# Third weight matrix: its sums made in the first pass, two stores left out, and an issue order tied

## The chip, the core and the metric

The kernel runs on one core of a Trainium2 chip. The metric is the device time of one execution in microseconds (us). Three timed runs of the kernel before gave 975.1, 977.63 and 981.88 us, median 977.63 us.

The engines named below: PE (TensorE matmul; PEld is its weight load), DVE (VectorE), ACT (ScalarE), POOL (GpSimd), and SP (SyncE), whose queue issues every transfer of this kernel. Each engine works through its own queue in order.

## The reference

Attention over 8 batches, 8 heads, 576 tokens, head size 64, with keys and values averaged over groups of 8 tokens; its output, as 4608 rows of 512, goes through a gated feed-forward layer of width 1536.

```
k_p, v_p = mean over 8 tokens of k, v
attn     = softmax(q @ k_p.T / sqrt(64))          # 72 keys per head
x        = (attn @ v_p) as [4608, 512]
gate     = sigmoid(x @ w_gate);  val = x @ w_val  # [4608, 1536] each
out      = (gate * val) @ w_out                   # [4608, 512]
```

## The kernel before, in words

**Numbers as pairs.** Every operand of a large product is split into a high part and the rest (`split`, L164): ACT copies to the rounded type, DVE subtracts. A product then takes three matmuls (high-high, rest-high, high-rest). The weights come as 64-bit words that `to_f32` (L179) turns into 32-bit floats with two ACT and three DVE instructions per tile.

**Blocks.** The 4608 rows are 12 blocks of 384. Blocks 0 and 1 are done in `first_pass` (L850 on) with plain products: `whole` (L631, PE line L645) for gate and value, `accumulate` (L1133) for the third product. Blocks 2 to 11 are done in five pairs with a scheme of seven products for eight, for which sums and differences of matrix quarters are needed, of weights as well as of x and of h. A pair runs through `hidden` (PE line L605: gate and value products, with the attention of the blocks after next between them) and then `second_sums` (PE line L825: the third product, 7 x 3 units).

**Weights on their way.** In the first pass each weight tile is loaded, converted and split; the parts are stored to device memory for the later pairs (`keep_parts` for gate and value, `keep_o` for the third matrix). `keep_parts` stores four quarter parts per tile pair, among them number 8, the parts of the quarter W12, which `reload` never reads: it counts `n = sum(m != 8 ...)`. The converted weights themselves are stored too (`keep_whole`, `keep_w`), because the sums of quarters are made from them later. For the third matrix this is `sums("O", p)` (L262 to L281), called for p = 0 to 5 in the first pair: it loads `keptwO` back (512 KB), makes four differences on DVE (L270 to L272), splits them in two halves (ACT L166, DVE L167) and stores four parts (`keptS`, 256 KB each). `second_sums` reads `keptO` and `keptS` back as its weights.

**What sets the order.** Inside `first_pass` the string `ORDER` is the program: each word is one step (`conv.0.2` one instruction of a weight conversion, `sc.0.1` the scores of block 0 and head pair 1, `keep`, `oconv`, `hshi`, `acc`, ...), and every engine's queue follows it. After it a scheduler orders each engine's queue by its own estimate of when things are ready; `in_turn` (L158), where `tied[0]` is set, pins an instruction behind everything written before it for its engine. In `second_sums` the generator `operands()` (L578) prepares the next pair's x: from unit 8 on, every second unit makes one of seven operands (addition L574, copy ACT L166, rest DVE L167). These are not pinned before, so the scheduler places them.

**Buffers.** `big` has four buffers of 8 KB per partition, in rotation: the 64-bit weight tiles, the third matrix's raw tiles (`load_o`), the first pass's split h (`hshi`, `hslo`), and its outputs. `opool` has four as well.

Of the kernel before, what the change touches and what calls it, by code (L numbers as in the profile page):

```python
# [65 lines left out]
vlo.1.0 max.0.1 first.1.0 conv.0.0 keys.1.0 first.0.2 conv.0.0 lr.1.0 lq.1.0 sc.0.0@1 conv.0.0 put.1.0 first.0.3
lk.1.1 first.1.2 keys.0.2 sc.1.0@2 exp.0.1 first.1.3 put.0.2 conv.0.0 sc.0.2@0 rsum.1.0 rhi.1.0 max.0.0 exp.0.0
lw.1.0 lq.1.1 first.2.0 first.3.0 keys.0.3 lk.1.2 put.0.3 lq.2.0 conv.0.0 conv.0.0 keys.1.1 put.1.1 sc.0.3@1 lw.0.1
lq.1.2 lr.1.1 max.0.2 lk.1.3 sc.1.1@3 sum.0.0 max.0.3 exp.0.2 rest.0.0 conv.0.0 main.0.1 conv.0.0 main.0.0
turn.0.0@0 rlo.1.0 conv.1.0 lv.1.1 lq.2.1 again.0.0 rturn.0.0@4 conv.1.0 conv.1.0 lq.1.3 turn.0.1@5 max.1.0 exp.0.3  # L70
keep.0.0 pv.0@6,7 sc.2.0@1 lk.3.1 hi.0.0 rcopy.0.0 max.1.1 exp.1.1 hi.0.1 exp.1.0 conv.1.0 vput.1.0 conv.0.1 sum.0.1
vhi.0.0 conv.1.0 kw.1.0 vhi.0.3 lo.0.0 main.0.2 rest.0.1 lo.0.1 keys.1.2 main.0.3 turn.0.3@5 sum.1.0 main.1.1
main.1.0 max.2.0 keys.1.3 again.0.1 rturn.0.1@2 rsum.1.1 turn.0.2@0 put.1.2 vhi.0.2 vlo.0.2 conv.0.1 conv.1.0
vhi.0.1 sc.1.2@3 vlo.0.0 lq.2.3 rcopy.0.1 kw.0.0 rhi.1.1 rest.1.0 put.1.3 vlo.0.3 vlo.0.1 hi.0.3 hi.0.2 sc.2.1@4
sc.1.3@2 exp.2.0 lw.1.1 turn.1.1@6 vsum.1.1 lo.0.3 lk.3.0 lq.2.2 av.0.0@1 conv.1.0 again.1.0 turn.1.0@5 max.1.2
exp.1.2 lo.0.2 conv.1.0 keep.1.0 sc.2.3@0 hi.1.0 max.1.3 keys.3.1 x.0.0 exp.1.3 lq.3.1 av.0.2@3 x.0.2 conv.0.1
av.0.3@1 x.0.3 av.0.1@7 x.0.1 rturn.1.0@2 sc.2.2@3 rcopy.1.0 max.2.1 keys.3.0 xhi.0.1 put.3.1 put.3.0 xhi.0.0 lq.3.0
lo.1.0 av.1.0@2 vhi.1.1 rlo.1.1 conv.1.1 x.1.0 vput.1.1 sum.1.1 main.1.2 lw.0.2 conv.0.1 lv.1.2 rest.1.1 again.1.1
xlo.0.1 sc.3.1@7 hi.1.1 sc.3.0@1 lv.1.3 xlo.0.0 vlo.1.1 conv.0.1 main.1.3 turn.1.3@5 hi.1.3 lv.3.3 lw.1.2 exp.2.1
V.0.0@2 lk.3.2 lo.1.1 rturn.1.1@6 conv.0.1 lo.1.3 vsum.1.2 conv.0.0 rcopy.1.1 sum.2.0 lr.3.0 keep.0.1 conv.0.1  # L80
turn.1.2@5 max.2.3 av.1.1@4 vhi.1.2 x.1.1 rest.2.0 conv.1.0 hi.1.2 lo.1.2 kw.0.1 conv.1.1 vput.1.2 keep.1.1 max.2.2
vlo.1.2 conv.0.1 conv.1.1 G.0.1@6 G.0.0@4 vsum.1.3 lw.0.3 conv.1.1 keep.0.2 main.2.0 main.2.1 exp.2.3 exp.2.2
conv.0.1 keep.0.3 again.2.0 V.0.1@5 conv.1.1 gate.0.1 conv.0.2 lv.3.0 av.1.2@0 x.1.2 vhi.1.3 h.0.1 conv.1.1 conv.0.2
G.0.2@3 gate.0.2 conv.1.1 conv.1.1 vlo.1.3 kw.1.1 G.0.3@6 turn.2.1@5 hi.2.1 vput.1.3 conv.1.1 keep.1.2 keep.1.3
lw.1.3 conv.0.2 rturn.2.0@3 rcopy.2.0 lo.2.1 vsum.3.3 V.0.2@0 conv.0.2 av.1.3@5 turn.2.0@3 gate.0.3 lq.3.2 V.0.3@6
x.1.3 conv.0.2 h.0.2 av.2.1@0 hi.2.0 lo.2.0 av.2.0@3 conv.0.2 conv.0.2 keep.0.4 G.0.4@5 xhi.1.0 sum.2.1 xlo.1.0
xhi.1.1 xlo.1.1 keys.3.2 x.2.1 conv.1.2 conv.1.2 rsum.3.0 main.2.2 turn.2.2@0 x.2.0 conv.1.2 G.1.0@3 conv.0.2
gate.0.0 h.0.3 conv.1.2 conv.0.3 h.0.0 hi.2.2 kw.0.2 lk.3.3 lw.0.4 conv.0.3 gate.0.4 gate.1.0 G.1.1@4 V.1.0@6
max.3.1 lv.3.2 conv.1.2 kw.1.2 G.1.4@3 rhi.3.0 rlo.3.0 rest.2.1 main.2.3 conv.1.3 turn.2.3@5 h.1.0 conv.1.2 conv.1.2
conv.0.3 conv.0.2 put.3.2 max.3.0 conv.0.3 conv.1.2 conv.1.2 lw.1.4 conv.0.3 keys.3.3 keep.0.5 conv.1.3 keep.1.4  # L90
kw.0.3 V.0.4@6 h.0.4 exp.3.1 conv.1.3 lo.2.2 V.1.2@2 exp.3.0 conv.0.3 conv.0.4 lw.0.5 keep.1.5 conv.0.3 put.3.3
keep.0.6 G.1.5@7 conv.1.3 again.2.1 vsum.3.0 conv.0.4 gate.1.5 vput.3.0 conv.0.4 conv.1.3 V.1.4@1 conv.0.4 gate.1.1
V.1.1@0 h.1.1 conv.0.3 conv.0.3 V.1.5@7 h.1.5 kw.1.3 conv.1.4 lw.1.5 conv.1.3 conv.1.4 rturn.2.1@4 conv.0.4 hi.2.3
conv.1.4 sum.3.0 main.3.1 conv.1.3 G.1.2@6 main.3.0 G.1.3@0 rcopy.2.1 av.2.2@4 gate.1.2 h.1.2 sc.3.2@6 V.1.3@7
conv.1.4 conv.0.5 gate.1.4 ol.0 G.1.7@2 x.2.2 conv.1.3 conv.1.3 vput.3.1 conv.1.4 h.1.4 V.1.7@4 conv.0.5 G.0.5@1
conv.0.4 conv.0.4 conv.0.4 conv.0.5 lv.3.1 conv.1.5 conv.0.5 lq.3.3 lr.3.1 vsum.3.2 kw.0.4 conv.1.4 gate.1.7 ol.1
conv.1.5 rsum.3.1 h.1.7 oconv.0 oconv.0 V.0.7@2 oconv.0 keep.0.7 turn.3.0@4 kw.1.4 vsum.3.1 vhi.3.3 vhi.3.2 sc.3.3@3
keep.1.6 rhi.3.1 keep.0.8 rlo.3.1 vhi.3.0 gate.1.3 conv.0.5 ol.2 vput.3.2 G.0.7@0 lo.2.3 gate.0.5 h.1.3 conv.1.5
av.2.3@7 oconv.1 conv.0.4 hi.3.0 vhi.3.1 rest.3.0 conv.1.4 oconv.1 keep.0.9 kw.0.5 turn.3.1@5 conv.0.5 conv.1.5
# [1137 lines left out]
```

## Time and profile before

| | |
|---|---|
| timed runs | 975.1, 977.63, 981.88 us; median 977.63 us |
| the profiled execution | 978.66 us; its span 976.9 us |
| busy, share of the span | PE 96%, PEld 93%, DVE 72%, ACT 57%, POOL 5% |
| transfers | 251.10 MB, 257 GB/s over the span |
| stages by PE's lines | first pass's products to about 256 us; then five times `hidden` and `second_sums` |

The profile page gives for each engine the busy time, and a strip of 40 slices. The timeline gives single instructions with the idle time of their engine before them and, behind an arrow, what ended that idle time. A row of the windows view gives the busy time of each engine in one stretch. A busy PE row hides gaps shorter than a matmul's overlap with the next, since a matmul's end is modelled.

### The profile page before, as it was taken

How to read it: one execution, taken by the hardware profiler on the slowest of the kernel's cores; microseconds unless marked ns; L12 is line 12 of the kernel's file. 1: busy time of each engine (PE TensorE's matmuls, PEld its weight loads, DVE VectorE, ACT ScalarE, POOL GpSimd, SP SyncE). 2: the span in 40 equal slices, each digit the busy share in tenths (PEclk: the TensorE clock that was granted, in tenths of full speed). 3: DMA queues.
4: the chain of work that ended last, by engine and by line, in shares of the span. 5: the costliest groups of instructions: out<-in, count | busy, mean ns of one | idle time of the engine just before them, and what ended most of it. 6: DMA issues, size and time to landing. Idle time of an engine off the chain costs nothing.

```text
span 976.9 us, 15387 instructions
## 1 busy us (share of the span) xinstructions
PE 940.9 (96%) x5412; PEld 906.5 (93%) x5412; DVE 700.8 (72%) x1221; ACT 553.6 (57%) x1138; POOL 51.8 (5%) x67
## 2 busy tenths in 40 slices
...
GB/s 313 305 300 337 353 359 243 175 150 262 289 394 336 196 235 255 371 382 324 127 211 283 276 222 270 195 170 242 293 266 205 217 123 230 285 243 251 164 210 221
DMA packets 115068, 251.10 MB, mean 257 GB/s; under 512 B 11952, under 2 KB 49584, under 8 KB 113456
## 3 DMA queue, kind: packets, MB, share of 16 engines
...
q8 instruction: 43, 0.70, 0.3%
q14 instruction: 33, 0.27, 0.1%
HBM read 193.45 MB, written 56.62 MB: 256 GB/s over the span
## 4 chain that ended last, share of the span: by engine, by line
PE 71%; DVE 13%; DMA 10%; ACT 4%; issue 2%; SPq 1%; POOL 0%; DVEq 0%; POOLq 0%; ACTq 0%
PE chain L605 35%; PE acc L825 18%; PE chain L645 7%; PE acc L1133 5%; PE av L447 2%; PE sc L438 2%; DMA raw<-in_kT 1%; DVE hs L789 1%; DVE s L757 1%; DMA raw_o<-in_wo 1%; DMA w<-keptwO 1%; DMA w<-keptwV 1%; PE tp L526 1%; DMA raw<-in_wgv 1%; DMA keptwV<-w 1%
## 5 line engine op out<-in xcount | busy, mean ns | idle before, releaser
L605 PE MATMUL chain<-xo,parts 128*128 128x384 f32 x2352 | 441.7, 341 | 5.8 <-ACT sG L611 1.8
L605 PEld LDWEIGHTS chain<-xo,parts 128*128 128x128 f32 x2352 | 409.6, 188 | 10.6 <-ACT sG L611 2.4
L825 PE MATMUL acc<-hs,oparts 128*128 128x384 f32 x1260 | 229.3, 336 | 3.7 <-DVE hs L789 3.0
L825 PEld LDWEIGHTS acc<-hs,oparts 128*128 128x128 f32 x1260 | 218.1, 188 | 6.7 <-DVE hs L789 4.6
L645 PE MATMUL chain<-xo,parts 128*128 128x384 f32 x552 | 102.2, 340 | 2.8 <-DVE xo L1086 1.4
L617 DVE TENSOR_TENSOR y<-chain,sG 128x384 f32<-128x384 f32 x84 | 46.1, 553 | 77.3 <-ACT sG L611 26.2
L645 PEld LDWEIGHTS chain<-xo,parts 128*128 128x128 f32 x552 | 96.1, 188 | 4.2 <-DVE xo L1086 1.6
L617 DVE TENSOR_TENSOR y<-chain,sV 128x384 f32<-128x384 f32 x84 | 46.1, 551 | 35.1 <-PE chain L605 22.9
L789 DVE TENSOR_TENSOR hs<-h,hs 128x768 fp32r<-128x768 f32 x60 | 58.3, 979 | 16.6 <-ACT hs L788 16.5
L623 ACT ACTIVATE gate<-y 128x384 f32<-128x384 f32 x84 | 43.9, 525 | 41.2 <-DVE y L617 40.8
L788 ACT CAST hs<-h 128x768 fp32r<-128x768 f32 x60 | 50.1, 835 | 29.9 <-PE acc L825 29.4
L611 ACT COPY sV<-chain 128x384 f32<-128x384 f32 x84 | 40.0, 476 | 45.3 <-PE chain L605 42.5
L611 ACT COPY sG<-chain 128x384 f32<-128x384 f32 x84 | 39.9, 476 | 44.8 <-PE chain L605 44.2
L520 POOL TENSOR_TENSOR pm<-e,rz 128x384 f32<-128x384 f32 x32 | 31.3, 979 | 601.9 <-DVE rz L500 347.2
L788 ACT CAST hs<-s 128x768 fp32r<-128x768 f32 x45 | 37.0, 835 | 29.6 <-PE acc L825 21.4
L438 PE MATMUL sc<-kbd,raw 128*128 128x144 f32 (+1 forms) x280 | 47.6, 306 | 3.4 <-DMA raw<-in_qT 2.5
L1133 PE MATMUL acc<-oparts,hs 128*128 128x512 f32 x216 | 50.7, 391 | 0.0
L626 DVE TENSOR_TENSOR h<-y,gate 128x384 f32<-128x384 f32 x84 | 46.9, 562 | 1.7
L789 DVE TENSOR_TENSOR hs<-s,hs 128x768 fp32r<-128x768 f32 x45 | 42.4, 954 | 7.8 <-ACT hs L788 7.6
L438 PEld LDWEIGHTS sc<-kbd,raw 128*128 128x128 f32 (+1 forms) x280 | 37.3, 184 | 11.3 <-issue 4.0
L1133 PEld LDWEIGHTS acc<-oparts,hs 128*128 128x128 f32 x216 | 40.3, 188 | 8.0
L645 PE MATMUL chain<-xo,parts_x 128*128 128x384 f32 x216 | 40.2, 337 | 0.0
...
## 6 DMA issues: line engine op xcount, KB each, us to landing
...
oparts<-keptO SPq DMA_DIRECT2D x90, 256.0 KB, 3.8
...
raw<-in_vm SPq DMA_DIRECT2D x28, 256.0 KB, 4.7
...
```

The source lines that it names most:

```text
L438: nc.tensor.matmul(sc[lo - i * P:hi - i * P, i], lhsT=q[:, lo:hi], rhs=kbd[slot(b, p)], start=True, stop=True)
L520: nc.gpsimd.tensor_tensor(out=pm, in0=e[:, n, :, :KM], in1=rz[:, n, :, None].broadcast_to([P, 2 * QT, KM]), op=ALU.mult)
L605: nc.tensor.matmul(t, lhsT=w[:, h, a], rhs=x[:, y, c], start=(m in (1, 2, 5) and c == 0 and k == 0), stop=(c == 1 and k == 2), skip_group_ ...
L611: nc.scalar.copy(s, t)
L617: nc.vector.tensor_tensor(out=y, in0=t, in1=seen[kind, {2: 1, 3: 6, 7: 5}[m]], op=ALU.add)
L623: nc.scalar.activation(gates[q[0]][:, q[1]], y, AF.Sigmoid)
L626: nc.vector.tensor_tensor(out=hb[f // 4][:, f % 4, q[0] * BT:(q[0] + 1) * BT], in0=y, in1=gates[q[0]][:, q[1]], op=ALU.mult)
L645: nc.tensor.matmul(t, lhsT=w[:, c // 2, h, a], rhs=x[:, y, c % 2], start=(c == 0 and k == 0), stop=(c == NC - 1 and k == 2),)
L788: nc.scalar.copy(hs[:, 0], x)
L789: nc.vector.tensor_tensor(out=hs[:, 1], in0=x, in1=hs[:, 0].bitcast(F32), op=ALU.subtract)
L825: nc.tensor.matmul(acc[name, c], lhsT=w[:, k, h, c * P:(c + 1) * P], rhs=hs[:, y, k], start=(m in (1, 2, 5) and i % 3 == 0 and k == 0 and ...
L1133: nc.tensor.matmul(acc[i], lhsT=hss[f][:, y, a], rhs=oparts[f][:, w], start=(f == 0 and k == 0), stop=(f == NF - 1 and k == 2),)
```

## The change

1. `ORDER` is replaced as a whole. It has new words `osum` (a step of the sums of the third matrix) and `keeps` (their four stores), and no `keepw`.
2. `summed_o` makes the third matrix's sums from the two raw tiles while they are still in their `big` buffers; its result is a new `big` tile. One ACT copy and one DVE subtraction of four quarters take the place of two and two. The calls of `sums("O", ...)` in the first pair are gone, and with them the store and reload of `keptwO`.
3. `keep_parts` leaves out part 8.
4. In `second_sums` the steps of `operands()` run with `tied[0]` set.

```
 ORDER = """
-first.0.1 first.0.0 keys.0.0 first.1.1 keys.0.1 put.0.0 put.0.1 sc.0.1@0 lv.1.0 lw.0.0 lk.1.0 vsum.1.0 vhi.1.0
+first.0.0 first.0.1 keys.0.1 put.0.1 lv.1.0 keys.0.0 put.0.0 first.0.3 vsum.1.0 vhi.1.0 first.1.1 sc.0.1@0 first.0.2
...
     def keep_parts(kind, f):
         for k, m in enumerate(CHUNK[f % 2]):
-            keep(kind, f // 2, m, plain[kind, f][:, k])
+            if m != 8:
+                keep(kind, f // 2, m, plain[kind, f][:, k])
...
-    def keep_w(f):
-        w = raws_o.pop(f)[:, 2 * DM:].bitcast(F32)
-        for half in range(2):
+    def summed_o(p):
+
+        first, raw = raws_o.pop(2 * p), raws_o.pop(2 * p + 1)
+        w11, w12 = (first[:, 2 * DM:].bitcast(F32)[:, h * HALF:(h + 1) * HALF] for h in range(2))
+        w21, w22 = (raw[:, 2 * DM:].bitcast(F32)[:, h * HALF:(h + 1) * HALF] for h in range(2))
+        s = raw[:, :2 * DM].bitcast(F32).rearrange("p (m n) -> p m n", m=4)
+        nc.vector.tensor_tensor(out=s[:, 0], in0=w12, in1=w11, op=ALU.subtract)
+        nc.vector.tensor_tensor(out=s[:, 1], in0=w22, in1=w12, op=ALU.subtract)
+        yield
+        nc.vector.tensor_tensor(out=s[:, 2], in0=w22, in1=s[:, 0], op=ALU.subtract)
+        nc.vector.tensor_tensor(out=s[:, 3], in0=w21, in1=s[:, 2], op=ALU.subtract)
+        yield
+        t = sums_o[p] = big.tile([P, 4, 2, HALF], F32R, name="sums", tag="big")
+        nc.scalar.copy(t[:, :, 0], s)
+        yield
+        nc.vector.tensor_tensor(out=t[:, :, 1], in0=s, in1=t[:, :, 0].bitcast(F32), op=ALU.subtract)
+        yield
+
+    def keep_sums(p):
+        for k, m in enumerate((5, 7, 6, 4)):
             nc.sync.dma_start(
-                kept_w["O", f // 2][:, (half, 3 - half)[f % 2]], w[:, half * HALF:(half + 1) * HALF]
+                kept_s[m, p // 2][:, p % 2].bitcast(F32), sums_o[p][:, k].rearrange("p h n -> p (h n)").bitcast(F32)
             )
...
-            if i in (2,3,):
-                tied[0] = True
-                sums("O", made_o.pop(0))
-                tied[0] = False
...
-                    if (p, i) in ((0, 3), (0, 8), (1, 1), (1, 8),):
-                        sums("O", made_o.pop(0))
...
             if i >= 8 and i % 2 == 0:
+                tied[0] = True
                 next(build, None)
+                tied[0] = False
```

What moves on the engines, at three places. Line numbers after the change are some 10 to 30 higher than before.

**DVE, start of the first pass.** `TENSOR_REDUCE early<-h` and `early<-raw` (L943, then L954) are sums of keys, `early<-sc` (L957, L968) a maximum of scores, `w` and `raw` of 1024 elements the conversion of a weight tile. Before:

```order
2 L943 TENSOR_REDUCE early<-h 128x72 x2
3 L381 TENSOR_REDUCE small<-raw 128x64
4 L1050 TENSOR_TENSOR vl_105<-small,vh_100 64x64 x2
5 L957 TENSOR_REDUCE early<-sc 128x6
6 L943 TENSOR_REDUCE early<-raw 128x72
7 L194 TENSOR_SCALAR w_262<-w_262 128x1024
8 L943 TENSOR_REDUCE early<-h 128x72
9 L196 SCALAR_TENSOR_TENSOR raw_251<-raw_251 128x1024
10 L381 TENSOR_REDUCE small<-raw 96x64
```

After:

```order
2 L954 TENSOR_REDUCE early<-h 128x72 x2
3 L397 TENSOR_REDUCE small<-raw 128x64
4 L954 TENSOR_REDUCE early<-h 128x72 x2
5 L968 TENSOR_REDUCE early<-sc 128x6
6 L397 TENSOR_REDUCE small<-raw 128x64
7 L968 TENSOR_REDUCE early<-sc 128x6
8 L954 TENSOR_REDUCE early<-raw 128x72
9 L397 TENSOR_REDUCE small<-raw 96x64
10 L968 TENSOR_REDUCE early<-sc 128x6
```

The four key sums and three maxima of block 0 come first, and the first weight tile's conversion comes later (row 20). In both kernels the two subtractions that finish block 0's split x (L1086 before, L1097 after) are DVE's 77th and 78th instruction. SP loads accordingly: the first 1 MB weight tile is its 6th transfer before and its 16th after.

**ACT, first pair's `hidden`, the middle of it.** `sums` is the split of a sum of the third matrix, `sG` and `sV` the copies that empty a bank of products. Before:

```order
320 L611 COPY sV_3493<-chain 128x384
321 L611 COPY sG_3360<-chain 128x384
322 L166 CAST parts<-w_3282 128x256
323 L529 CAST ph<-tp 128x384
324 L166 CAST parts<-w_3149 128x256
325 L166 CAST sums<-s_3257 128x2x256
326 L611 COPY sG_3403<-chain 128x384
327 L166 CAST parts<-w_3282 128x256
```

After:

```order
332 L627 COPY sG_3288<-chain 128x384
333 L167 CAST parts<-w_3210 128x256
334 L410 ACTIVATE kbd_92<-ks 64x72
335 L639 ACT_TABLE_LOAD
336 L639 ACTIVATE gate_3342<-y 128x384
337 L167 CAST parts<-w_3093 128x256
338 L797 CAST hs<-h 128x768
339 L627 COPY sG_3331<-chain 128x384
340 L167 CAST parts<-w_3210 128x256
```

The twelve `sums` copies of the third matrix stand in this stretch before and none of them after; six copies of four quarters stand in the first pass instead. What the scheduler puts between the other instructions is different too: here a copy of h (`hs`) and a table load.

**DVE, third `second_sums` (the pair of blocks 6 and 7).** `hs` is the rest of an operand of the third products, `s_...<-h` and `h<-h` the additions for it; `s<-xs` (L574, then L590) an addition of x and `xo` the rest of an operand made of it. Before:

```order
863 L757 TENSOR_TENSOR s_7249<-h 128x768
864 L574 TENSOR_TENSOR s<-xs_6470 128x768
865 L757 TENSOR_TENSOR h<-h 128x2x384
866 L484 TENSOR_REDUCE m<-sc 128x6
867 L789 TENSOR_TENSOR hs<-s_7249,hs 128x768
868 L789 TENSOR_TENSOR hs<-s_6597,hs 128x768
869 L487 TENSOR_TENSOR e<-sc,m 128x432
870 L381 TENSOR_REDUCE ks<-raw 128x72
871 L789 TENSOR_TENSOR hs<-s_6597,hs 128x768
872 L167 TENSOR_TENSOR xo_7448<-s,xo_7448 128x768
873 L757 TENSOR_TENSOR s_7249<-s_7249,h 128x768
874 L757 TENSOR_TENSOR s_6597<-h,s_6597 128x768 x2
```

After:

```order
867 L798 TENSOR_TENSOR hs<-s_6525,hs 128x768
868 L766 TENSOR_TENSOR s_6525<-h,s_6525 128x768 x2
869 L798 TENSOR_TENSOR hs<-s_7177,hs 128x768
870 L798 TENSOR_TENSOR hs<-h,hs 128x768
871 L766 TENSOR_TENSOR s_7177<-h,s_7177 128x768
872 L798 TENSOR_TENSOR hs<-h,hs 128x768
873 L168 TENSOR_TENSOR xo_7333<-xs_6026,xo_7333 128x768
874 L798 TENSOR_TENSOR hs<-h,hs 128x768
875 L798 TENSOR_TENSOR hs<-s_6525,hs 128x768
876 L590 TENSOR_TENSOR s<-xs_6398 128x768
877 L798 TENSOR_TENSOR hs<-s_6525,hs 128x768
878 L812 TENSOR_TENSOR o<-acc,sG_7211 128x384
```

Before, the first addition of x stands at the head of the stage; after the change it stands behind more than eight operands of h, and the last operands of x (rows 897 and 898) stand behind the last outputs that DVE writes in the stage.

## Rows read from the trace of the kernel before

**Rows 1.** The page's head: span, then busy time, share and count of each engine

```profile
span 976.9 us, 15387 instructions
PE 940.9 (96%) x5412; PEld 906.5 (93%) x5412; DVE 700.8 (72%) x1221; ACT 553.6 (57%) x1138; POOL 51.8 (5%) x67
```

**Rows 2.** Windows: length, busy us of PE, PEld, DVE, ACT, POOL; clock, DMA

```profile
0.00:53.60 53.60, 32.15 (x171) 25.53 (x171) 41.80 (x79) 40.71 (x131) 10.59 (x27) 0.97 0.92 313
53.60:75.00 21.40, 20.91 (x130) 19.97 (x131) 19.27 (x35) 16.49 (x42) 1.86 (x2) 1.00 0.83 287
...
75.00:100.00 25.00, 24.77 (x143) 24.00 (x142) 24.82 (x39) 24.14 (x47) 2.83 (x2) 1.00 0.98 340
...
175.00:200.00 25.00, 25.00 (x128) 22.20 (x127) 15.11 (x22) 12.80 (x21) 0.00 (x0) 1.00 0.37 122
...
250.00:325.00 75.00, 73.21 (x441) 70.54 (x440) 70.90 (x152) 53.87 (x122) 8.12 (x6) 1.00 0.96 339
325.00:400.00 75.00, 75.00 (x447) 74.73 (x447) 64.38 (x102) 44.58 (x84) 3.32 (x4) 1.00 0.71 235
```

**Rows 3.** PE's waits over the whole span: engine, line, tile, releaser: us, times, longest

```profile
PE acc L825 <- DVE hs L789: 3.0, 5, 1.0
```

**Rows 4.** Timeline of PE to 57 us: start, us, instruction, idle before and its releaser

```profile
12.17 1.81 PE L438 MATMUL sc<-kbd,early 128*128 128x144 f32 x6 [2.03 <-DMA early<-in_qT]
...
53.60 2.21 PE L645 MATMUL chain<-xo,parts 128*128 128x384 f32 x11 [1.39 <-DVE xo L1086]
```

**Rows 5.** Timeline of DVE to 54 us, three of its idle times

```profile
2.63 0.28 DVE L140 CAST identr<-cst 128x128 fp32r<-128x128 f32 x1 [2.63 <-DMA cst<-in_const]
...
5.03 1.41 DVE L943 TENSOR_REDUCE early<-h 128x72 f32<-128x576 f32 x2 [2.11 <-DMA h<-in_kT]
...
45.85 0.75 DVE L943 TENSOR_REDUCE small<-raw 128x72 f32<-128x576 f32 x1 [2.47 <-DMA raw<-in_kT]
```

**Rows 6.** Groups by line: operation, tiles, shapes, count, busy us, mean ns, idle before

```profile
L270 DVE TENSOR_TENSOR s<-w 128x512 f32<-128x512 f32 x10 | 6.9, 687 | 6.1 <-DMA w<-keptwO 4.8 <-DMA w<-keptwV 1.3
...
L271 DVE TENSOR_TENSOR s<-w,s 128x256 f32<-128x256 f32 x10 | 4.8, 481 | 0.1
...
L272 DVE TENSOR_TENSOR s<-w,s 128x256 f32<-128x256 f32 x10 | 4.2, 417 | 0.0
...
L167 DVE TENSOR_TENSOR sums<-s,sums 128x512 fp32r<-128x512 f32 x20 | 14.2, 713 | 0.9 <-ACT sums L166 0.9
...
L166 ACT CAST sums<-s 128x512 fp32r<-128x512 f32 x20 | 12.4, 621 | 13.4 <-DVE s L270 3.7 <-DVE m L484 3.0 <-issue 2.4
...
L196 DVE SCALAR_TENSOR_TENSOR raw<-raw 128x1024 uint32<-128x1024 uint32 x12 | 14.7, 1228 | 0.0
...
L188 ACT ACTIVATE w<-raw 128x1024 f32<-128x1024 f32 x12 | 13.9, 1156 | 1.6 <-DMA raw<-in_wgv 1.6
...
L1133 PE MATMUL acc<-oparts,hs 128*128 128x512 f32 x216 | 50.7, 391 | 0.0
```

**Rows 7.** Timeline of ACT, then of PE, around 300 us, first pair's hidden stage

```profile
300.01 0.62 ACT L166 CAST sums<-s 128x512 fp32r<-128x512 f32 x1 [0.89 <-DVE s L270]
...
301.06 1.15 PE L605 MATMUL chain<-xo,parts 128*128 128x384 f32 x5 [1.33 <-ACT sG L611]
```

**Rows 8.** DMA issues: tiles, queue, count, KB each, median us to landing

```profile
keptS<-sums SPq DMA_DIRECT2D x24, 256.0 KB, 5.4
```

**Rows 9.** Timeline of DVE from 648 us, third pair's `second_sums`

```profile
649.74 0.95 DVE L574 TENSOR_TENSOR s<-xs 128x768 f32<-128x768 f32 x1
...
652.05 1.82 DVE L789 TENSOR_TENSOR hs<-s,hs 128x768 fp32r<-128x768 f32 x2
...
659.30 0.96 DVE L574 TENSOR_TENSOR s<-s,xs 128x768 f32<-128x768 f32 x1
```

**Rows 10.** Timeline from 200 us: last raw tile's load on SP, end of its conversion on DVE

```profile
200.55 0.33 SPq L311 DMA_DIRECT2D raw_o<-in_wo  x1
...
210.19 0.69 DVE L320 TENSOR_TENSOR oparts<-raw_o,oparts 128x512 fp32r<-128x512 f32 x1
```

More of the change, by code (lines that the diff above doesn't have):

```diff
@@ L64 @@
 ORDER = """
-first.0.1 first.0.0 keys.0.0 first.1.1 keys.0.1 put.0.0 put.0.1 sc.0.1@0 lv.1.0 lw.0.0 lk.1.0 vsum.1.0 vhi.1.0
[L66 to L99, printed above, removed]
@@ new lines @@
+conv.0.0 lw.0.1 rest.0.1 lo.0.0 lq.1.2 keys.1.3 kw.0.0 lr.1.1 rcopy.0.0 again.0.1 conv.1.0 main.0.2 main.0.3
+rturn.0.1@4 turn.0.3@3 conv.1.0 vhi.0.1 lq.2.1 vhi.0.3 sc.1.1@1 lq.2.2 hi.0.3 vhi.0.0 vhi.0.2 lo.0.1 conv.1.0
+rcopy.0.1 sc.2.0@0 keys.1.2 lk.3.1 put.1.2 conv.1.0 sc.1.2@4 vlo.0.3 lw.1.1 conv.0.1 conv.0.1 turn.0.2@2 conv.1.0
+put.1.3 vlo.0.0 max.1.1 exp.1.1 lo.0.3 keep.0.0 vlo.0.2 conv.0.0 max.1.2 vlo.0.1 keep.0.1 hi.0.2 rsum.1.1 max.2.0
+exp.1.2 conv.1.0 lq.3.0 sum.1.0 main.1.0 kw.1.0 main.1.1 av.0.0@3 sc.1.3@7 sc.2.2@1 sc.2.1@4 max.1.3 lq.2.3 put.3.0
@@ new lines @@
+h.1.0 G.1.2@7 conv.1.2 sc.3.2@1 conv.0.2 keep.0.5 keep.1.4 lo.2.2 G.1.5@0 rcopy.2.1 h.1.3 conv.0.3 kw.0.3 V.1.2@4
+keys.3.3 lo.2.3 av.2.3@2 av.2.2@5 conv.1.2 conv.1.2 conv.1.3 lq.3.3 exp.3.1 sum.3.0 conv.0.4 lv.3.2 V.1.5@6 conv.0.4
+conv.1.3 conv.0.3 lw.0.5 conv.0.3 keep.0.6 conv.1.3 rhi.3.1 conv.1.4 conv.0.3 keep.1.5 lw.1.5 gate.1.2 G.0.5@7 h.1.2
+rest.3.0 conv.0.4 conv.0.4 x.2.3 main.3.0 conv.1.3 conv.1.4 conv.0.3 V.1.4@2 turn.3.0@4 gate.1.5 conv.0.4 again.3.0
+keep.0.7 rturn.3.0@0 gate.1.4 x.2.2 main.3.1 turn.3.1@5 conv.0.5 ol.0 h.1.5 kw.0.4 conv.1.4 conv.0.5 G.0.4@6 h.1.4
```

82 lines of the change are left out of this document (53 added, 29 removed).

## The prediction, made before the changed kernel ran

> **What bounds the kernel now.** Read the page's head first [rows 1]: PE is busy 940.9 of 976.9 us, so at most 36.0 us of visible idle time can be won as long as the products stay the same, and they do: the change adds and removes no matmul. The question is where those 36.0 us lie and which of them the change reaches. The windows view, read by stage [rows 2], answers the first half. The first 53.6 us hold 21.45 of them, the 21.4 us behind those 0.49, 75 to 100 us 0.23; between 250 and 325 us there are 1.8, between 325 and 400 none. The list of PE's waits [rows 3] has, for the second half of the program, 3.0 us for h's operands (DVE), in five places of at most 1.0.
>
> In the start PE waits for DVE. The first product gets going at 53.60 us, released by the split of x on DVE [rows 4]. DVE was busy 41.80 of the 53.60 us before that [rows 2], so it stood idle for 11.8. Two views show where: 2.63 and 2.11 us for the first constants and the first k, 2.47 for a late k at 45.85 us [rows 5], the rest in small pieces, among them waits for scores, which PE made late because q landed behind other loads (2.03 us at 12.17 us, [rows 4]).
>
> **The change part by part.**
>
> *Start of the first pass: taken at -3.0 us, bounds -6 and +2.* The split of x is DVE's 77th and 78th instruction in both orders, and the mix is the same but for one more split of a 512-wide weight part, like the 0.71 us of L167 [rows 6], and one short instruction less: 0.5 more. So DVE's work ahead of PE's first product stays; what can change is its idle time. The first two k land as before, so 2.63 + 2.11 = 4.7 us stay. Then two more k and three q come before the first weight tile, and key sums and maxima of block 0 follow one another; of the other 7.1 us I leave 2.7, an estimate: some for the third k and the first maxima, the rest for the small gaps. That is 4.4 us less idle, less 0.5 more work: 3.9 if no wait like the 2.47 comes back, 1.4 if it does. Behind the start PE cannot run ahead at will: DVE is busy 24.82 of 25 us between 75 and 100 us [rows 2], with the same work per product. I take 3.0. The largest gain, -6, is nearly all of the 7.1 us, less the 0.5; the other bound, +2, is one new wait of the size seen (2.47) with no gain elsewhere but 0.5. The first weight tile comes later in SP's queue (16th, not 6th); its first ACT instruction (L188, [rows 6]) then stands in ACT's queue behind the exponentials of block 0, which do not need it, and before the second group's, which would be late if it were.
>
> *Rest of the first pass: 0, bounds -1 and +3.* The twelve stores of part 8 and the 24 stores of `keptwO` go from SP's queue; the 24 stores of `keptS` (256 KB, 5.4 us to landing, [rows 8]) come into it. None is on PE's path. DVE gets six sums: four subtractions of 256 elements at 0.42 to 0.48, 1.8 us, and a subtraction of 1024, bounded by 0.70 for 512 and 1.23 for another operation of 1024 [rows 6]; I take 1.2, since it is the same length. ACT gets six copies of 1024 at about 1.16 (L188, [rows 6]). That is 18 us of DVE and 7 us of ACT, at a time when there is room: between 175 and 200 us DVE was busy 15.11 and ACT 12.80 of 25 us, and transfers 0.37 [rows 2]. The cover is thin at one point, the last raw tiles, and this is the slower rival below.
>
> *Sums out of the first pair: taken at -2.5 us, bounds 0 and -4.2.* Six sums leave the stretch of 236 to 326 us: on DVE 6 x (0.69 + 0.48 + 0.42 + 2 x 0.71) = 18.1 us, on ACT 12 x 0.62 = 7.4 us [rows 6], and on the transfer queues 6 loads of 512 KB and 24 stores of 256 KB, 9.4 MB, while the transfers were busy 0.96 of the time [rows 2]. DVE was busy 70.90 of 75 us there; with about 15 of the 18 us gone it has less than the 64.38 of the next 75 us, in which PE never stood. What PE lost can be pointed at: at 300.01 us ACT begins a `sums` copy after 0.89 us of waiting for DVE's L270, the copy `sG` that empties a bank stands behind it, and PE idles 1.33 us [rows 7]. That is three quarters of the stretch's 1.8 us. PE's busy rows hide short gaps, though. Weight loads were busy 70.54 of 75 us in this stretch and 74.73 in the next, where the products have the same shape [rows 2]: by this the loss is 74.73 - 70.54 = 4.2 us. I take 2.5, between the two, because the queue of ACT after the change has new instructions in front of `sG`, as the order shows. What is late next, once DVE has room, is the bank copies behind PE itself. A table load more on ACT for each of two tables costs nothing while ACT is busy 54 of 75 us.
>
> The Trainium skill, in Trainium Kernel Development and Optimization, section Performance Expectations, says that matmul busy time is a bad measure of how close PE is to its limit, since matmuls are pipelined, and that the busy share of weight loads is the good one. By it this term would be -4.2 and the sum 1.7 us lower. The trace agrees in this stretch; in the whole span the rule would find 976.9 - 906.5 = 70.4 us, of which a part is not idle at all, as the third product of the first pass streams 512 columns per load.
>
> *x's additions tied: taken at -2.0 us, bounds -3.0 and +2.* Of PE's waits for h's operands (3.0 us in five places, [rows 3]) one is plain in DVE's timeline: before the `hs` at 652.05 us stands an addition of x of 0.95 us at 649.74, and another, of 0.96, at 659.30 among the next ones [rows 9]. Tied, all of them stand behind these operands, as the order shows. I take two thirds of the 3.0 because the last pair has no x to prepare and its waits stay. What the tie adds is a wait at the other end: the last operands of x are made after the stage's last outputs, and `hidden` of the next pair reads them. An operand costs an addition of 0.95 us, a rest of 0.91 (half of the 1.82 at 652.05, same shape, [rows 9]) and a copy on ACT of at most the 1.16 of 1024 elements [rows 6]; its first reader in `hidden` is PE's sixth product, some 6 us in, so I cost it nothing. If that cover were gone it would be up to 0.5 us at each of four borders, the +2.
>
> *What the scheduler does elsewhere: 0, within 2 us either way.* The later pairs keep their sums of gate and value, and the stretch from 325 to 400 us had nothing to lose to them [rows 2].
>
> *Sum.* -3.0 + 0 - 2.5 - 2.0 = -7.5. The profiled execution took 978.66 us (span 976.9), 1.0 above the median of the runs. 978.66 - 7.5 = 971.2; against the median, **970.2 us**.
>
> **Rivals.**
>
> *A. The start gives nothing.* DVE is filled to the limit from 50 to 100 us, and another late load stands in for the 2.47. For it: SP's queue is in order, and every move of a load delays others; against it: the q of block 0 are now ahead of all weights. Start 0, the rest as forecast, a little less: -4. Time 978.66 - 4 - 1.0 = 973.7. Chance 0.2.
>
> *B. PE loses more than its busy rows show, and gets it back.* By the weight loads the first pair's stretch gives 4.2, the start its full 3.9, the tie all 3.0, and scheduling chance 1: -12.1. For it: 74.73 against 70.54 [rows 2]; against: it needs all terms at their ends. Time 978.66 - 12.1 - 1.0 = 965.6. Chance 0.22. The Trainium skill's rule on weight loads, named above, is the rule behind it.
>
> *C. Slower: the raw tiles come late at the end of the first pass.* The sums now need a `big` buffer of their own, held until four stores land (5.4 us), and both raw tiles of a pair stay until the sums have read them. In rotation the 12th raw tile gets the buffer of h's ninth operand, so its load starts when PE has finished with that. From there PE has 36 matmuls of the third product at 50.7 / 216 = 0.235 us [rows 6], 8.5 us, and some 12 shorter ones, at most 2.8, before it needs the tile: 8.5 to 11.3 us, of which I take 10.7. Before, load and conversion of this tile took from 200.55 to 210.88 us, 10.3 us [rows 10]. Now a sum's 3.0 us of DVE and 1.2 us of ACT may stand in front. The 11th tile waits for stores to land as well. The point that decides is whether the chain exceeds 10.7 us: if a sum (3.0 + 1.2) and its stores (5.4) all come into it, PE waits 9.6 us. With the start at 0 and 2.5 us won later, 978.66 + 9.6 - 2.5 - 1.0 = 984.8. Against it: the order puts the last sum behind most of the conversion. Chance 0.08.
>
> **The numbers.** Forecast 970.2 us, chance 0.5, itself spread over 967 to 973. The range of 8 in 10 reaches from 964 (B and its half spread) to 978 (A and its half, short of C): **964 to 978**. One per cent, 9.8 us, is about what a measurement of this kernel can tell from no change. Below 967.9 lie most of B (0.19) and the lower end of the forecast (0.08): 0.27. Above 987.4 lies the upper end of C: 0.03. Within: 0.70.
>
> **What would show it.** In the changed profile the start is right if PE's first plain product starts near 50 us and DVE's idle time before it is near 7 us; wrong if a new DMA wait of over 2 us stands there. The sums are right if PE's idle time between 250 and 325 us is under 0.5 us and DVE's share there falls to that of the later pairs; the tie, if waits of line L825 (new number) for `hs` fall to about 1 us and no wait for `xo` appears at the border to `hidden`. A PE wait for `oparts` or `hs` before the first outputs, near 205 to 215 us, would be C. The prediction would be wrong altogether if the first products of blocks 0 and 1 were starved after 55 us: then several us of idle time would stand in the 21 us behind the first product, where 0.49 stood.

## The result, and the profile after

The changed kernel takes 982.41 us (median of 15 runs, 980.55 to 986.88); the kernel before, run on the same chip, 978.44 us (15 runs). The ratio is 1.003, with a 95% interval of 1.0016 to 1.0044: slower by 1.6 to 4.3 us, where 7.5 us less was forecast, and above the range's end of 978. (The medians differ by 4.0 us, the ratio says 2.9: it is not the quotient of the two medians.) The profiled execution took 982.51 us.

The page's head, beside [rows 1]:

```profile
span 980.7 us, 15323 instructions
PE 945.8 (96%) x5412; PEld 912.5 (93%) x5412; DVE 706.2 (72%) x1221; ACT 558.3 (57%) x1134; POOL 46.9 (5%) x67
```

PE's matmuls are as many, and it is "busy" for 4.9 us more. So more busy time does not mean less lost time here; part of the loss is inside it. The windows say where, beside [rows 2] (columns as there):

```profile
0.00:53.60 53.60, 35.51 (x179) 30.52 (x180) 45.64 (x82) 40.62 (x126) 9.21 (x27) 0.88 0.94 325
53.60:75.00 21.40, 20.71 (x133) 20.18 (x132) 19.99 (x39) 20.00 (x51) 4.09 (x4) 0.98 0.80 270
75.00:100.00 25.00, 25.00 (x150) 24.91 (x149) 22.63 (x34) 21.37 (x43) 2.83 (x2) 1.00 0.80 277
...
250.00:325.00 75.00, 71.33 (x423) 69.00 (x422) 54.74 (x122) 44.77 (x106) 4.99 (x6) 0.98 0.65 209
325.00:400.00 75.00, 75.00 (x447) 74.72 (x446) 63.13 (x101) 49.21 (x87) 4.08 (x4) 1.00 0.70 226
```

From 250 to 325 us DVE fell from 70.90 to 54.74 us and transfers from 0.96 to 0.65, as forecast, and yet PE did 423 matmuls where it had done 441. The list of PE's waits (engine, line, tile, releaser: us, times, longest) has new entries, and the one of [rows 3] is nearly gone:

```profile
PE chain L621 <- ACT gate L639: 2.3, 1, 2.3
...
PE chain L621 <- DMA parts<-keptG2B: 2.0, 2, 1.7
PE chain L621 <- DMA parts<-keptG3B: 1.8, 2, 1.5
...
PE acc L834 <- DVE hs L798: 0.3, 1, 0.3
```

PE now waits for weights (`keptG2B`, `keptG3B`) that it hardly waited for before, and for a gate on ACT.

**PE's lost time by stage.** To see losses shorter than a visible gap, and those of a slower clock, I took from each trace the time from one matmul's start to the next one's, less the usual time for that shape (the lower quartile over all profiles of this study), and added it up by stage. "hid" is a pair's `hidden`, "sec" its `second_sums`; "0-60" holds all time before PE's first matmul too. us:

```
                        0-60 60-h1  hid1  hid2  hid3  hid4  sec3  sec4 other  total  profiled time
before                  33.1   5.6   5.2   8.3   3.8   3.4   3.6   1.7   6.3   70.9  978.66
before, again (e14)     32.0   5.5   4.8   8.0   3.5   4.0   3.6   1.7   5.7   68.7  976.48
changed                 31.4   6.4   8.5   7.5   7.7   6.1   0.4   0.6   6.1   74.8  982.51
changed, again (e13)    30.0   6.6   7.5   7.5  11.3   6.5   0.4   0.6   6.0   76.5  984.23
e1 tie only             34.0   8.7   5.1   8.4   7.4   6.9   0.4   1.0   7.9   79.8  987.66
e2 untied               31.2   5.1   7.5   6.6   5.6   4.7   3.2   1.7   6.2   71.9  979.57
e3 sums again           29.6   6.4   3.9   9.7   4.0   6.9   0.4   0.6   7.1   68.7  976.36
e4 stores on POOL       30.8   5.9   5.7   7.5   9.9   5.8   0.4   0.6   5.2   71.9  980.08
e5 two stores           30.4   6.5   6.8   8.2   7.7   6.2   0.4   0.6   9.5   76.4  984.07
e6 two stores, untied   29.8   7.1   7.6   7.3   6.3   4.7   3.6   1.7   6.3   74.5  982.18
e7 again, untied        30.5   6.1   4.6  13.4   4.6   3.8   3.6   1.7   6.7   74.9  982.62
e8 no part 8            34.5   4.5   4.3   8.1   3.7   3.7   3.2   1.7   6.0   69.8  977.48
e16 no part 8, again    31.3   4.5   4.3   8.0   3.9   3.2   3.2   1.7   6.7   66.8  974.48
e9 one unit earlier     30.9   4.5   8.8   8.7   3.4   6.1   0.4   0.5   6.1   69.3  977.06
e10 earlier, no part 8  30.2   3.8   4.0   7.0   5.2   5.7   0.6   0.7   8.4   65.7  973.40
e11 part 8 stored       30.2   9.0   7.7   7.5   8.0   5.9   0.4   0.6   6.1   75.4  983.28
e12 earlier, POOL       31.0   5.3   4.8   7.9   3.8   7.1   0.8   0.5   6.2   67.4  975.58
e15 earlier, POOL again 31.2   4.9   5.5   7.9   3.7   7.2   0.7   0.6   8.1   69.7  977.83
```

Read the first four rows. The change wins about 2 us before 60 us and 4.3 in the third products of pairs 3 and 4. It loses 3 us in the first pair's `hidden`, and 6 to 10 in those of pairs 3 and 4, whose own code the diff leaves as it was. A row is one execution: the kernel before and e1 have the same order on PE, DVE and ACT up to 255 us, and yet lost 5.6, 5.5 and 8.7 us from 60 us to the first pair.

### The profile page after: what moved, and what is told of

The parts are those of the page before. It is cut to its first block, busy times and chain, and to the rows that moved or that the text cites. A ratio compares the mean times of both kernels' runs of the same rounds, so it can differ in the third digit from the quotient of the medians.

```text
span 980.7 us, 15323 instructions
## 1 busy us (share of the span) xinstructions
PE 945.8 (96%) x5412; PEld 912.5 (93%) x5412; DVE 706.2 (72%) x1221; ACT 558.3 (57%) x1134; POOL 46.9 (5%) x67
## 4 chain that ended last, share of the span: by engine, by line
PE 71%; DVE 12%; DMA 10%; ACT 5%; issue 2%; SPq 1%; DVEq 0%; ACTq 0%
PE chain L621 34%; PE acc L834 21%; PE chain L661 7%; PE acc L1149 3%; PE sc L454 3%; PE av L463 3%; DMA out<-o 2%; DMA parts<-keptG2B 1%; PE tp L542 1%; DVE raw L197 1%; DVE w L199 1%; DMA raw<-in_kT 1%; DMA parts<-keptG3B 1%; DVE parts L239 1%; DMA parts<-keptG4B 1%
## 5 line engine op out<-in xcount | busy, mean ns | idle before, releaser
L536 POOL TENSOR_TENSOR pm<-e,rz 128x384 f32<-128x384 f32 x32 | 29.1, 910 | 636.1 <-DVE rz L516 378.7
L797 ACT CAST hs<-s 128x768 fp32r<-128x768 f32 x45 | 37.3, 837 | 29.6 <-PE acc L834 22.0
```

Source lines behind the costliest of these rows:

```text
L797: nc.scalar.copy(hs[:, 0], x)
```

## The experiments

Medians, with the ratio to the kernel before on the same chip. Differences in the text are those of the ratios, times 978.4 us. Each interval reaches 1.2 to 2.5 us to either side, so two versions that differ by less than some 2 us are not told apart.

```
                        median us   ratio    95% interval
changed                  982.41    1.0030   1.0016 to 1.0044
e1 tie only              985.36    1.0076   1.0050 to 1.0102
e2 untied                979.16    1.0005   0.9992 to 1.0018
e3 sums again            976.31    0.9972   0.9954 to 0.9990
e4 stores on POOL        981.19    1.0034   1.0022 to 1.0046
e5 two stores            981.07    1.0021   1.0004 to 1.0037
e6 two stores, untied    980.29    1.0009   0.9996 to 1.0022
e7 again, untied         982.94    1.0050   1.0032 to 1.0068
e8 no part 8             974.91    0.9958   0.9939 to 0.9977
e9 one unit earlier      977.95    0.9996   0.9982 to 1.0010
e10 earlier, no part 8   976.45    0.9968   0.9951 to 0.9984
e11 part 8 stored        986.22    1.0080   1.0058 to 1.0102
e12 earlier, POOL        977.85    0.9993   0.9978 to 1.0008
```

**e1: the kernel before with the tie alone.**

```
             if i >= 8 and i % 2 == 0:
+                tied[0] = True
                 next(build, None)
+                tied[0] = False
```

> The kernel before with x's additions tied, nothing else. Theory (the tie moves waits: h's operands come earlier in the third products, the next pair's first gates later): same as before within 2 us, 976.5 to 980.5; PE's waits for hs fall from 3.0 to under 1 us, and 2 to 4 us of new waits stand in the first 20 us of a later hidden stage. Rival 1 (my prediction's term): 2 us faster, 976.5 or less. Rival 2 (the tie is what made the changed kernel slower): 981.5 to 983.

7.4 us slower: rival 2, and by more than it said (its profile has a bad first pass besides, which the tie doesn't touch). The waits for `hs` went (sec3 3.6 to 0.4), and hid3 and hid4 lost 3.6 and 3.5 more. In hid3 PE waits 2.3 us for a gate on ACT, as in the changed kernel: the tie alone makes that wait.

**e2: the changed kernel without the tie** (those two lines taken out).

> The changed kernel with the tie undone. Theory (the loss arises in the first pair's hidden stage, where the tie does not act): still 2 to 4 us above before, 980.5 to 983; PE still loses 3 to 5 us more than before between 280 and 325 us. Rival (the tie costs it): 977 to 979.5.

Level with before: the rival's time, though the theory's stage, hid1, still lost 7.5. The tie costs the changed kernel 2.4 us. PE's waits for `keptG2B` and `keptG3B` are there without it too, 1.9 and 1.7 us.

**e3: six sums made a second time in the first pair**, at their old places in `hidden` and `hidden_second`:

```
+                    if (p, i) in ((0, 3), (0, 8), (1, 1), (1, 8),):
+                        sums("G", made_o.pop(0), "O")
```

> The changed kernel, with six sums put back into the first pair's hidden stage at their old places: same loads (512 KB, of the gate's stored quarters), same additions, splits and stores (256 KB, to a tile that nothing reads), on top of the sums in the first pass. Theory (taking the work out made the scheduler put stores that wait for DVE ahead of weight loads in SP's queue; with the work back the loads come first again): not slower than the changed kernel in spite of 18 us more DVE work, 978 to 982, SP's waits for DVE parts fall from 25 us towards the 11 us of before. Rival (less work in that stage is a gain, the loss has another cause): 984 to 987.

DVE is busy for 15 us more (721.4 against 706.2), and the kernel is 5.7 us faster than the changed one, 2.7 faster than before: more than the theory had said. A part of this comes from SP's queue. Its issues in the changed kernel (start, us, tile):

```profile
280.20 0.38 SPq L297 DMA_DIRECT2D parts<-keptG2A  x1
282.83 0.32 SPq L213 DMA_DIRECT2D keptG2A<-parts  x1
283.81 0.32 SPq L213 DMA_DIRECT2D keptV1D<-parts  x1
284.18 0.44 SPq L254 DMA_DIRECT2D w<-keptwV  x1
284.70 0.42 SPq L297 DMA_DIRECT2D parts<-keptG2B  x1
...
301.21 0.40 SPq L297 DMA_DIRECT2D parts<-keptG3A  x1
303.97 0.32 SPq L213 DMA_DIRECT2D keptG3A<-parts  x1
306.44 0.32 SPq L213 DMA_DIRECT2D keptV2D<-parts  x1
306.85 0.38 SPq L297 DMA_DIRECT2D parts<-keptG3B  x1
```

And in e3:

```profile
276.37 0.33 SPq L305 DMA_DIRECT2D parts<-keptG2A  x1
278.28 0.33 SPq L213 DMA_DIRECT2D keptG2A<-parts  x1
279.66 0.33 SPq L305 DMA_DIRECT2D parts<-keptG2B  x1
...
294.79 0.32 SPq L305 DMA_DIRECT2D parts<-keptG3A  x1
295.20 0.39 SPq L213 DMA_DIRECT2D keptV2C<-parts  x1
297.33 0.32 SPq L305 DMA_DIRECT2D parts<-keptG3B  x1
297.74 0.39 SPq L213 DMA_DIRECT2D keptG3A<-parts  x1
```

And in the kernel before:

```profile
298.14 0.38 SPq L300 DMA_DIRECT2D parts<-keptG3A  x1
299.76 0.32 SPq L300 DMA_DIRECT2D parts<-keptG3B  x1
300.97 0.32 SPq L212 DMA_DIRECT2D keptG3A<-parts  x1
...
302.82 0.38 SPq L212 DMA_DIRECT2D keptV2D<-parts  x1
```

`parts<-keptG3B` loads a weight, `keptG3A<-parts` stores a new part that DVE must first finish. In e3, as in the kernel before, this load goes ahead of the stores of `keptG3A` and `keptV2D`, and follows `keptG3A`'s load by 2.5 us (1.6 before); in the changed kernel both stand in front, and it follows by 5.6. Between 230 and 335 us SP stood 25.2 us before stores that waited for DVE's splits of weight parts, in e3 6.2, in the kernel before 11.4. The scheduler makes this order from its own estimate of when DVE is done. PE then met the late loads (timeline: start, us, instruction, idle before and releaser):

```profile
290.64 2.38 PE L621 MATMUL chain<-xo,parts 128*128 128x384 f32 x12 [1.67 <-DMA parts<-keptG2B]
...
310.50 6.96 PE L621 MATMUL chain<-xo,parts 128*128 128x384 f32 x30 [1.46 <-DMA parts<-keptG3B]
```

The second profile of the changed kernel has both again, 2.1 and 1.5 us. In e3 neither wait is there and hid1 loses 3.9. But hid1 is not the whole of the 5.7 us: hid3 lost 4.0 in e3 against 7.7 and 11.3, and the gate wait that is told under e9 is not there either. And the 5.7 us hold only with the tie; see e7.

**e4: those stores on POOL's queue, in the changed kernel.**

```
-            keep(kind, p, GROUPS[g][i], t[:, i])
+            keep(kind, p, GROUPS[g][i], t[:, i], nc.gpsimd)
```

> The changed kernel with the stores of the first pair's new weight parts (256 KB each, made from sums of quarters) issued on POOL's queue and no longer on SP's. Theory (weight loads stand in SP's queue behind stores that wait for DVE): PE's waits for keptG2B and keptG3B (3.1 us) and the stretch at half clock behind them go, 3 to 5 us faster than the changed kernel, 977.5 to 979.5. Rival 1 (the loads are late because their buffers come free late or because transfers are slow): 981.5 to 983.5, the two waits stay. Rival 2 (POOL's own work for the attention is held up by the stores): 984 or more, PE waits for pm.

The waits went as the theory said: PE's list from 250 to 332 us has left

```profile
PE chain L621 <- ACT sV L627: 0.6, 1, 0.6
PE chain L621 <- DVE y L633: 0.3, 1, 0.3
PE chain L621 <- DMA parts<-keptG2B: 0.3, 1, 0.3
PE chain L621 <- ACT sG L627: 0.2, 1, 0.2
```

and hid1 lost 5.7 (4.8 and 5.5 in e12 and its repeat, with 0.6 and 1.2 us of waiting for `keptG2B` left). The time did not follow: 1.0034 against 1.0030. In its profile hid3 lost 9.9, some of it in a stretch partly at half clock (granted 0.76 and 0.81 from 552 to 560 us). So the cause of the two waits is shown; what they are worth in the end is not, and lies below what was expected. Whether the stores cost something elsewhere on POOL's queue was not tested apart.

**e5, e6: two stores pinned behind two loads**, written one reload later; e6 untied as well.

```
+        store = keep(kind, p, m, t)
+        if (kind, p, place(m)[0]) in (('V', 1, 'D'), ('V', 2, 'D')):
+            tc.keep_in_program_order(store)
```

> The changed kernel with the stores of the first pair's new parts written one reload later, and two of them (keptV1D, keptV2D) pinned in SP's queue behind the weight loads (of keptG2B, keptG3B) that they precede in the changed kernel. Hardly anything else moves: 12 places each on DVE and ACT, 9 on SP. Theory (these two loads stand behind stores that wait for DVE, and the two PE waits of 3.1 us and the half clock behind them are what the first pair lost): 3 to 5 us faster than the changed kernel, 977.5 to 979.5; PE's waits for keptG2B and keptG3B under 0.5 us each. Rival (the loads are late for another reason, or PE meets the next wait at once): 981 to 983.5.

> The same two stores pinned, and the tie of x undone as well. Theory (two causes that add: the stores 3 us, the tie 3 us of the kernel's time): 975 to 977. Rival (what the tie costs is not the tie but the order that the scheduler happens to find after any edit; 178 places on DVE differ from the untied kernel): anywhere from 976 to 983, with lost time in later stages that neither of the two kernels shows.

Neither theory held. In e5 PE still waited 1.46 us for `keptG2B` and 1.16 for `keptG3B`: the loads passed the two stores, but the stores of `keptG2A` and `keptG3A` and the 512 KB load of `keptwV` were still in front of them, and the store of `keptV2C` now stood between the loads of `keptG3A` and `keptG3B`. e5 won 0.9 us and e6 came out 0.4 above e2, both within the intervals: the times of their rivals.

**e7: e3 without the tie.**

> The kernel with the six sums made twice (first pass and first pair, 976.3 us), with the tie undone. Theory (the tie by itself costs 3 us, at the border to the next hidden stage and in it): 972 to 974. Rival (the tie gains in the third products and loses at the borders by what the scheduler makes of it, no price of its own): 975 to 979.

7.6 us slower than e3, past both. Without the tie sec3 is back at 3.6, and hid2 lost 13.4: PE waited 1.62 us for `keptG2B` there, and then ran partly at half clock (1.2 GHz; windows, columns as in [rows 2]):

```profile
388.00:392.00 4.00, 1.86 (x6) 1.54 (x7) 2.46 (x6) 1.06 (x4) 0.00 (x0) 0.86 0.99 383
392.00:396.00 4.00, 4.00 (x18) 4.00 (x18) 3.15 (x6) 2.12 (x4) 0.00 (x0) 0.71 1.03 363
```

So the tie has no price of its own: it gave 7.6 us here, cost 2.4 in the changed kernel and 7.4 in e1. Nor has making the sums a second time: with the tie it gave 5.7 us (e3 against the changed kernel), without it it cost 4.4 (e7 against e2). What comes back both times is hid1's loss: 3.9 and 4.6 with the sums there, 7.5 to 8.5 without.

**e8 and e11: part 8 left out of the kernel before, and stored in the changed one.**

```
     for k, m in enumerate(CHUNK[f % 2]):
-        keep(kind, f // 2, m, plain[kind, f][:, k])
+        if m != 8:
+            keep(kind, f // 2, m, plain[kind, f][:, k])
```

> The kernel before without the twelve stores of part 8 (256 KB each), nothing else; the first pass's order on PE, DVE and ACT is the same, and later 10 places on DVE and 7 on ACT differ. Theory (the stores are hidden): same as before, 978 to 980. Rival (with transfers busy 1.00 of the time from 100 to 150 us, loads come earlier): 975 to 977.

> The changed kernel with the twelve stores of part 8 put back at their places in the first pass; PE's order is the same, on DVE 4 places differ. Theory (leaving the stores out is worth what it was worth alone, 4 us): 985 to 988. Rival (they are hidden, and the 4 us are the order of later stages): 981 to 983.5.

4.1 us won and 4.9 lost, e8's rival and e11's theory: the same price from both sides, with nearly the same order on PE, DVE and ACT. Twelve stores whose data nothing reads cost 4 us. In the stage table they account for 1 us (5.6 and 5.5 to 4.5) and 2.5 (6.5 to 9.0) between 60 us and the first pair. By the three profiles of the old order with these stores (5.6, 5.5, and e1's 8.7) and the three without (4.5, 4.5, and e10's 3.8) it is 2.3 in the mean; the rest is not in a stage that I can name. How a store costs this is not shown: fuller transfers and SP's in-order queue are both open. 60 to 150 us, changed kernel and then e11, in which PE did 14 matmuls fewer:

```profile
60.00:150.00 90.00, 88.72 (x530) 87.31 (x529) 83.30 (x138) 74.27 (x149) 6.92 (x6) 1.00 0.85 294
```

```profile
60.00:150.00 90.00, 87.17 (x516) 85.12 (x517) 82.30 (x136) 72.41 (x147) 7.44 (x6) 1.00 0.91 319
```

**e9: tied operands of x one unit earlier, in the changed kernel.**

```
-            if i >= 8 and i % 2 == 0:
+            if i >= 7 and i % 2 == 1:
```

> The changed kernel with the tied operands of x made one unit earlier (after units 7, 9, ... 19 of the third products and not 8, 10, ... 20), so that the last one stands ahead of the stage's last outputs and not behind them. Theory (the tie wins 4 us of waits in the third products of pairs 3 and 4 and loses 6 to 7 us in the hidden stages behind them, because the last operand and with it the next softmax are pinned behind the last outputs): third products of pairs 3 and 4 keep their low loss (0.4 and 0.6 us), the hidden stages of pairs 3 and 4 fall from 7.7 and 6.1 us towards 4 each; 976.5 to 979. Rival (any tie moves the softmax's table loads between the gates, wherever the last operand stands): 981 to 984, hidden stages as before.

3.3 us faster than the changed kernel, level with before. hid3 fell to 3.4 as the theory said, hid4 stayed at 6.1 as the rival said. ACT at the border between pair 2's third products and pair 3's `hidden`, in the changed kernel:

```profile
541.72 1.00 ACT L810 COPY o<-acc 128x384 f32<-128x384 f32 x2 [5.20 <-PE acc L834]
542.62 0.84 ACT L167 CAST xo<-xs 128x768 fp32r<-128x768 f32 x1
...
552.70 1.28 ACT L508 ACT_TABLE_LOAD   x1 [1.63 <-DVE e L503]
553.99 0.92 ACT L508 ACTIVATE e<-e 128x864 f32<-128x864 f32 x1
554.93 1.28 ACT L639 ACT_TABLE_LOAD   x1
556.23 0.49 ACT L639 ACTIVATE gate<-chain 128x384 f32<-128x384 f32 x1
```

In the kernel before:

```profile
533.62 1.28 ACT L492 ACT_TABLE_LOAD   x1
534.91 0.93 ACT L492 ACTIVATE e<-e 128x864 f32<-128x864 f32 x1
...
539.56 1.00 ACT L801 COPY o<-acc 128x384 f32<-128x384 f32 x2 [0.72 <-PE acc L825]
...
543.99 1.28 ACT L623 ACT_TABLE_LOAD   x1
```

DVE and PE there in the changed kernel:

```profile
543.49 0.96 DVE L168 TENSOR_TENSOR xo<-xs,xo 128x768 fp32r<-128x768 f32 x1 [6.35 <-ACT xo L167]
...
556.77 3.42 PE L621 MATMUL chain<-xo,parts 128*128 128x384 f32 x18 [2.30 <-ACT gate L639]
```

Before, the softmax's exponential (`e`) is done ahead of the last outputs, in the third products, where ACT has time. Tied, DVE first has to make the last operand of x, which waits 6.35 us for ACT's copy, itself behind the outputs. The softmax comes after it, its exponential falls between two gates, and two table loads of 1.28 us with it. PE's gate wait of 2.3 us is this. In e9 the exponential stands at 544.91, ahead of the first gates, and that wait is gone. All profiles bear it out: of the seven that are tied at the old units six have this wait, of 2.3 us each (not e3, where the scheduler put the exponential behind the first three gates); of the others, untied or one unit earlier, none has it.

**e10, e12: the versions that this pointed to.** e10 is e8 with the tie of e9, e12 is e9 with the stores of e4.

> The kernel before without the stores of part 8, and with x's operands tied one unit earlier. Theory (two gains that add: 4 us for the stores as measured, 3 to 4 us for the third products): 970 to 973. Rival (the tie's gain is given back in the hidden stages): 975 to 979.

> The changed kernel with x's operands one unit earlier, and the stores of the first pair's new parts on POOL's queue. Theory (both places of loss mended: 3 us in the first pair's hidden stage, 4 to 5 us behind the third products of pairs 2 and 3): 973 to 976. Rival (the order that the scheduler finds decides): 977 to 983.

Both theories were too good, and both rivals' ranges held. e10 has the lowest total of all profiles and the lowest single run (971.25), but its ratio is 1.0 us above e8's, which the intervals do not tell apart: by the table the third products' gain was given back in hid3 and hid4. e12 is no faster than e9, so moving the stores to POOL won no time here either.

**e13 to e16: second profiles.**

> The changed kernel once more, for a second profile. Theory (the loss in the first pair's hidden stage belongs to the order): that stage loses 6 to 9 us again, the hidden stages of pairs 3 and 4 together 12 to 15, the start up to 60 us 30 to 31.5. Rival (it was the one stretch at half clock): the first pair's stage loses 5 to 6.

> The kernel before once more, for a second profile. Theory: the first pair's hidden stage loses 5 us again, pairs 3 and 4 about 3.6 each, the start 33 to 34.5 us, so 2 to 3 more than the changed kernel's. Rival (the start differs by execution, not by order): under 31.5.

> The kernel with operands one unit earlier and stores on POOL once more. Theory (its first profile, 2 us below its median, was one of its best executions by its start): the first pair's hidden stage loses 4.5 to 6 again. Rival (the stores on POOL gain nothing there): 7.5 to 9.

> The kernel before without the stores of part 8 once more. Theory (the stores cost the first pass 2 to 3 us behind its start): 60 us to the first pair loses 4 to 5 us, against 5.6 and 8.7 with the stores; its time 973 to 977. Rival (the gain is elsewhere): above 5.5.

In the first four rows of the table a stage's loss comes back within 1 us, except 0-60 and hid3. hid1 is 8.5 and 7.5 against 5.2 and 4.8: it belongs to the order. hid3, 11.3, took pairs 3 and 4 together above their range: after the same gate wait PE's granted clock was 0.84 and 0.73 in two windows of 4 us (an estimate from these shares: at most 1.7 us lost), and it waited 1.3 us for `kbd` and 1.4 for `keptV1B`, where the first profile has 0.3 for `keptV1B` and no such wait for `kbd`. e15 and e16 came back as their theories said (hid1 5.5; 60-h1 4.5). The start's 32.0 against 31.4 and 30.0 lies between theory and rival: over all profiles the old order's start is 30.2 to 34.5 (mean 32.5 of six), the new one's 29.6 to 31.4 (30.6 of twelve).

The lowest ratio is that of e8, the kernel before without the stores of part 8 (974.91 us); its interval overlaps those of e10 and e3.

## Why the prediction was wrong

By the runs, everything but the tie came to +0.5 us (e2), where -5.5 was forecast, and the tie added 2.4, where it was to win 2.0. The two terms that failed most are the sums and the tie.

**Start, taken at -3.0: the right sign, about two thirds of the size.** By the profiles it is worth 1.9 us. The first product came at 50.31 us, near the 50 that was named, and DVE's idle time before 53.60 us fell from 11.8 to 53.60 - 45.64 = 8.0, near the 7 that was named. But the 3.3 us between 53.60 and 50.31 are not all gain. In the kernel before the product's first matmul ran earlier, and [rows 4] show the other eleven:

```profile
51.79 0.42 PE L645 MATMUL chain<-xo,parts 128*128 128x384 f32 x1
```

Its first matmul came only 1.5 us earlier. What was left out besides: scores come in fewer, later groups, PE stands longer between them (3.7 us for a q at 16.94 us, where the longest such wait was 2.0), and its granted clock in the first 53.6 us is 0.88, where it was 0.97.

**Rest of the first pass, taken at 0: two terms that hide each other.** The stores of part 8 were costed at nothing, "None is on PE's path"; left out, they give about 4 us by the runs (e8, e11). Against that, without part 8 the new order loses 5.9 us from 60 us to the first pair (mean of eleven profiles), the old one 4.5, 4.5 and 3.8. That the transfers stood at 0.98 of the time from 75 to 100 us was in [rows 2], a reason not to take the stores for free in the bounds of this term.

**Sums out of the first pair, taken at -2.5: the wrong sign in its stage, and the first step that failed.** The cover and the counts were right: DVE fell by 16 us and the wait for `sG` of [rows 7] shrank from 1.33 to 0.54 us. But the term took the order for fixed where the scheduler makes it: with less work on DVE, its estimate let stores go ahead of weight loads in SP's queue, and PE waited for those. Measured: +3 us in hid1 in the profiles, and they go when the stores leave the queue (e4) or the work comes back (e3, e7). "What is late next" was sought in the bank copies behind PE; it was behind SP, the queue from which the change took 6 loads and 24 stores. What this is worth in the whole kernel stays open: moving the stores won no time (e4, e12), and the work put back won or lost with the tie.

The rule of the Trainium skill on the busy share of weight loads (Trainium Kernel Development and Optimization, Performance Expectations) would have made this term 1.7 us better still. In this stretch weight loads went from 70.54 to 69.00 us and matmuls from 73.21 to 71.33, so both tell the loss; over the span both rose, 906.5 to 912.5 and 940.9 to 945.8, in a kernel that got slower.

**x's additions tied, taken at -2.0, bounds -3 and +2: the gain was right, the border was not, and this is the other step that failed.** The waits for `hs` went from 3.0 to 0.3 us, and sec3 and sec4 won 4.3 us, more than the list of waits had shown. The other end was named ("a wait at the other end") and priced at 0.5 us a border for the operand alone. What stood behind the operand in the queues, the softmax with two table loads, was not priced (a table load was put at nothing while ACT has room): hid3 lost 4 to 8 us and hid4 2.5. e9 shows it for hid3, where one unit's shift took 3.3 us off the whole kernel. What hid4 loses in every tied kernel (5.7 to 7.2 against 3.2 to 4.7 untied) stays open.

**The scheduler elsewhere, 0 within 2: too narrow.** e6 differs from e2 in two pinned stores, and 178 places on DVE changed; e3 and e7 differ by the tie, and hid2 by 3.7 us. An edit here is worth its own effect plus several us of whatever order follows from it.

Rival C's place stayed quiet (0.8 us for `hs` at 179 us). The losses came from two rivals that weren't listed: an in-order queue, in which a store that waits holds back a load, and a softmax that a pinned operand holds back.
